# Sign words of float64 weights on GpSimd: high words times 0.0 in place of a comparison

## The chip, the core and the metric

The kernel runs on one core of a Trainium2 chip. The metric is the device time in microseconds (us) of one execution. The engines are TensorE (PE, with its weight loads as PEld), VectorE (DVE), ScalarE (ACT), GpSimd (POOL) and SyncE (SP), which issues nearly all DMAs. Each engine takes its instructions in the order in which they stand in its own queue.

## The reference

```python
scores = q @ k.T / sqrt(64)                    # 4 batches x 8 heads, 576 x 576, head_dim 64
bias   = -(cum[:, None] - cum[None, :])        # cum: running sum of max(s, 0)
scores = where(causal, -1e9, scores + minimum(bias, 0))
x   = softmax(scores) @ v                      # to 2304 tokens x 512
h   = x @ w_in;  x = (h * clip(h + 3, 0, 6) / 6) @ w_out        # 512 -> 2048 -> 512
h   = x @ w2_in; out = (h / (1 + exp(-h))) @ w2_out             # 512 -> 2048 -> 512
```

The four weight matrices arrive as float64. [...]

## The kernel before, in words

Attention runs by head: 22 heads are done "whole" in one float32 matmul, the others with operands split into a high part and a remainder. Each of the two feed-forward layers multiplies with split operands as well: a product is high*high + high*low + low*high, three matmuls in a row (lines 260 to 262 and 299 to 301 in the first layer, 1013 to 1015 and 1029 to 1031 in the second).

Weights come in chunks of 128 x 512 values, two `in` and `out` chunks (`i`, `o`) for each of 16 slices of a layer. A `Chunk` goes through these steps: `load` (L147, a DMA of 128 x 1024 words into the tile `raw`); `fields`, where ACT shifts the low word (L159) and makes the magnitude (L160, tile `mag`, three buffers) and POOL makes the sign word in place of the high word (L161); `join`, where DVE shifts the magnitude and sets the sign (L172) and adds the low word (L176); then the split in a high part (ACT, L120) and a remainder (DVE, L187, which frees the `mag` buffer). All 64 chunks take L161. The high words that it reads and writes lie 8 bytes apart, since low and high words alternate in `raw`. For the `i` chunks of the second layer `Two` takes two chunks together, forms sums of them (L915), splits these too (L925, L927) and stores all in DRAM.

The first layer's gates are on ACT (L272) and DVE (L273), the high part `gh` of the gated values is a copy on POOL (L114) or, at the start, on DVE (L122), and its remainder `gl` is DVE's (L280). In the second layer DVE adds partial products (L1079, tiles `u` and `h`) out of the accumulator banks that PE then writes anew.

The program has three stretches that matter here: an opening (up to about 150 us), in which attention heads and the first layer's weight chunks share DVE and PE; the body, in which PE is fed without a break; and the change from the first layer to the second (about 540 to 650 us), in which DVE prepares the second layer's weights beside the last gates.

The order of instructions within each engine isn't the order of the code. A scheduler replays the whole program with its own cost for each instruction and fixes the queues by that. So a cheaper or dearer instruction moves others, on all engines.

Of the kernel before, what the change touches and what calls it, by code (L numbers as in the profile page):

```python
# [14 lines left out]
ALU = mybir.AluOpType  # L15
# [4 lines left out]
SIGN = -(2**31)  # L20


def f32(ap):
    return ap.bitcast(F32)
# [3 lines left out]
def kernel(  # L28
# [59 lines left out]
    def heads_of(x):  # L88
# [8 lines left out]
        out=cmask[:, NZ:], in_=cmask[:, NZ:], pattern=[[-1, P]],  # L97
# [32 lines left out]
    class Chunk:  # L130
# [20 lines left out]
        def fields(self):  # L151

            self.mag = stage.tile([P, DM], I32, tag="mag", name=f"mag{self.nm}")
            if self.src.dtype == F32:
                nc.scalar.copy(f32(self.mag), self.val)
                self.val = f32(self.mag)
                return
            low, high = self.words
            nc.scalar.activation(low, low.bitcast(U32), AF.Copy, scale=2.0**-29)  # L159
            nc.scalar.activation(f32(self.mag), f32(high), AF.Abs, scale=2.0**-112)  # L160
            nc.gpsimd.tensor_scalar(  # L161
                out=high, in0=f32(high), scalar1=0.0, scalar2=float(SIGN),
                op0=ALU.is_lt, op1=ALU.mult,
            )

        def join(self):
# [166 lines left out]
    def bank(kind, shape, name):  # L333
# [11 lines left out]
        out=srow, in0=srow, scalar1=0.0, scalar2=1.0 / SCALE, op0=ALU.max, op1=ALU.mult  # L345
# [876 lines left out]
```

## Time and profile before

| what | value |
|---|---|
| three runs, median (lowest to highest) | 1017.48 us (1015.5 to 1018.98) |
| the profiled execution | 1021.31 us, its span 1019.5 us |
| mean granted clock of TensorE | 0.991 of full speed |
| busy: PE, PEld, DVE, ACT, POOL | 989.4, 912.1, 715.0, 521.3, 340.5 us |
| L161 on POOL | 64 instructions, 69.5 + 68.8 us |

The span runs from the first instruction to the last; 1.8 us of the profiled execution lie around it. Busy time is the sum of an engine's instructions without overlaps. Matmul ends are modelled, so a PE that reads as busy can still run below its best rate; the number of matmuls in a stretch shows more. Spans on POOL are rough.

### The profile page before, as it was taken

How to read it: one execution, taken by the hardware profiler on the slowest of the kernel's cores; microseconds unless marked ns; L12 is line 12 of the kernel's file. 1: busy time of each engine (PE TensorE's matmuls, PEld its weight loads, DVE VectorE, ACT ScalarE, POOL GpSimd, SP SyncE). 2: the span in 40 equal slices, each digit the busy share in tenths (PEclk: the TensorE clock that was granted, in tenths of full speed). 3: DMA queues.
4: the chain of work that ended last, by engine and by line, in shares of the span. 5: the costliest groups of instructions: out<-in, count | busy, mean ns of one | idle time of the engine just before them, and what ended most of it. 6: DMA issues, size and time to landing. Idle time of an engine off the chain costs nothing.

```text
span 1019.5 us, 18411 instructions
## 1 busy us (share of the span) xinstructions
PE 989.4 (97%) x6404; PEld 912.1 (89%) x6404; DVE 715.0 (70%) x1724; ACT 521.3 (51%) x1144; POOL 340.5 (33%) x446
## 2 busy tenths in 40 slices
PE   8988989999999999999999999899999999999997
PEld 5788989999999999999998887789988999888996
DVE  5798998878778888887737799867574334743343
ACT  5798655555556566566526565546353232532232
POOL 7376754453245444444415366423000000000000
PEclk9998999999999999999999999999999999999999
DMA  4686112212312322322114965443354341432411
GB/s 153 197 286 225 38 37 83 74 57 59 91 57 65 92 58 68 94 59 67 59 42 136 380 247 175 146 186 114 145 189 165 132 144 74 177 137 110 145 73 62
DMA packets 52068, 124.80 MB, mean 122 GB/s; under 512 B 10004, under 2 KB 31752, under 8 KB 48648
## 3 DMA queue, kind: packets, MB, share of 16 engines
q1 hardware_dynamic: 51528, 122.97, 35.6%
q8 instruction: 51, 0.84, 0.3%
q10 hardware_dynamic: 448, 0.66, 0.2%
q14 instruction: 41, 0.34, 0.1%
HBM read 98.96 MB, written 24.63 MB: 121 GB/s over the span
## 4 chain that ended last, share of the span: by engine, by line
PE 78%; DVE 12%; ACT 3%; DMA 2%; POOL 2%; issue 2%; DVEq 0%; POOLq 0%; ACTq 0%; SPq 0%
PE a L1029 6%; PE a L1030 6%; PE a L1031 6%; PE h L1013 5%; PE h L1014 5%; PE h L1015 5%; PE acc L300 5%; PE ph L260 5%; PE acc L301 5%; PE acc L299 5%; PE ph L262 5%; PE ph L261 5%; PE poB L617 4%; PE pt0B L567 1%; DVE mago L172 1%
## 5 line engine op out<-in xcount | busy, mean ns | idle before, releaser
L300 PE MATMUL acc<-gl,wo 128*128 128x256 f32 (+1 forms) x512 | 155.0, 304 | 2.7 <-DVE gl L280 2.7
L260 PE MATMUL ph<-xh,wi 128*128 128x256 f32 (+1 forms) x512 | 152.8, 299 | 3.4 <-DVE g L273 3.4
L301 PE MATMUL acc<-gh,wo 128*128 128x256 f32 (+1 forms) x512 | 152.7, 300 | 0.0
L262 PE MATMUL ph<-xh,wi 128*128 128x256 f32 (+1 forms) x512 | 151.3, 296 | 0.6 <-DVE wi L187 0.6
L261 PE MATMUL ph<-xl,wi 128*128 128x256 f32 (+1 forms) x512 | 150.9, 295 | 0.0
L299 PE MATMUL acc<-gh,wo 128*128 128x256 f32 (+1 forms) x512 | 145.2, 301 | 3.1 <-DVE gh L122 3.1
L1071 ACT ACTIVATE gh<-h 128x384 fp32r<-128x384 f32 x96 | 50.3, 524 | 187.7 <-DVE h L1079 187.6
L1029 PE MATMUL a<-wo,gh 128*128 128x512 f32 x288 | 113.5, 394 | 2.6 <-ACT gh L1071 2.5
L1030 PE MATMUL a<-wo,gh 128*128 128x512 f32 x288 | 113.5, 394 | 0.0
L300 PEld LDWEIGHTS acc<-gl,wo 128*128 128x128 f32 x512 | 97.9, 191 | 8.1 <-DVE gl L280 4.9
L260 PEld LDWEIGHTS ph<-xh,wi 128*128 128x128 f32 x512 | 97.0, 190 | 7.1 <-DVE g L273 2.3
L299 PEld LDWEIGHTS acc<-gh,wo 128*128 128x128 f32 x512 | 96.4, 191 | 7.1 <-ACT magi L160 2.5
L301 PEld LDWEIGHTS acc<-gh,wo 128*128 128x128 f32 x512 | 97.9, 191 | 3.6
L262 PEld LDWEIGHTS ph<-xh,wi 128*128 128x128 f32 x512 | 97.0, 189 | 3.8 <-DVE wi L187 0.8
L261 PEld LDWEIGHTS ph<-xl,wi 128*128 128x128 f32 x512 | 96.9, 189 | 2.9
L161 POOL TENSOR_SCALAR rawi<-rawi 128x512 int32<-128x512 f32 x32 | 68.8, 2150 | 76.9 <-ACT magi L160 57.1
L1031 PE MATMUL a<-wo,gl 128*128 128x512 f32 x288 | 90.0, 393 | 0.3 <-DVE gl L1073 0.3
L161 POOL TENSOR_SCALAR rawo<-rawo 128x512 int32<-128x512 f32 x32 | 69.5, 2176 | 44.2 <-ACT mago L160 41.1
L1073 DVE TENSOR_TENSOR gl<-h,gh 128x384 fp32r<-128x384 f32 x96 | 53.6, 558 | 40.7 <-ACT h L1072 39.1
L1079 DVE TENSOR_TENSOR h<-h,u 128x384 f32<-128x384 f32 x72 | 40.1, 557 | 54.8 <-PE h L1015 54.6
L273 DVE SCALAR_TENSOR_TENSOR g<-g,ph 128x512 f32<-128x512 f32 (+1 forms) x76 | 49.5, 652 | 34.5 <-ACT g L272 34.3
L272 ACT ACTIVATE g<-ph,half 128x512 f32<-128x512 f32 (+1 forms) x76 | 50.3, 662 | 37.9 <-PE ph L262 37.2
(232 smaller groups left out, 2655.8 us busy)
## 6 DMA issues: line engine op xcount, KB each, us to landing
w<-w_d SPq DMA_DIRECT2D x18, 1792.0 KB
w_d<-w SPq DMA_DIRECT2D x8, 1792.0 KB
k2B<-in_kT_dram SPq DMA_DIRECT2D x64, 144.0 KB
rawi<-in_w1i_dram SPq DMA_DIRECT2D x16, 512.0 KB
rawo<-in_w1o_dram SPq DMA_DIRECT2D x16, 512.0 KB
rawi<-in_w2i_dram SPq DMA_DIRECT2D x16, 512.0 KB
rawo<-in_w2o_dram SPq DMA_DIRECT2D x16, 512.0 KB
q2B<-in_qT_dram SPq DMA_DIRECT2D x64, 80.0 KB
```

The lines of the kernel that those rows point to most:

```text
L161: nc.gpsimd.tensor_scalar(out=high, in0=f32(high), scalar1=0.0, scalar2=float(SIGN), op0=ALU.is_lt, op1=ALU.mult,)
L260: nc.tensor.matmul(o, wih[:, cs], xh[c], start=c == 0, stop=False)
L261: nc.tensor.matmul(o, wih[:, cs], xl[c], start=False, stop=False)
L262: nc.tensor.matmul(o, wil[:, cs], xh[c], start=False, stop=c == NDC - 1)
L299: nc.tensor.matmul(a, woh[:, cs], gh[:, jj, :], start=b0, stop=False)
L300: nc.tensor.matmul(a, woh[:, cs], gl[:, jj, :], start=False, stop=False)
L301: nc.tensor.matmul(a, wol[:, cs], gh[:, jj, :], start=False, stop=b1)
L1013: nc.tensor.matmul(ps, w[:, 0, cs], xh[:, c, :], start=c == 0, stop=False)
L1029: nc.tensor.matmul(accs[t], gh[:, k, cs], woh, start=b0, stop=False)
L1030: nc.tensor.matmul(accs[t], gh[:, k, cs], wol, start=False, stop=False)
L1031: nc.tensor.matmul(accs[t], gl[:, k, cs], woh, start=False, stop=b1)
L1073: nc.vector.tensor_tensor(out=gl[:, i, o], in0=g, in1=f32(gh[:, i, o]), op=ALU.subtract)
```

## The change

One instruction changes its arithmetic and its output type. Before, it compared the high word, read as float32, with 0.0 and multiplied the outcome by -2^31, written as an integer. Now it multiplies the high word by 0.0 and by 1.0 and writes float32: a zero that keeps the sign, whose bit pattern is the same sign word.

```diff
             nc.gpsimd.tensor_scalar(
-                out=high, in0=f32(high), scalar1=0.0, scalar2=float(SIGN),
-                op0=ALU.is_lt, op1=ALU.mult,
+                out=f32(high), in0=f32(high), scalar1=0.0, scalar2=1.0,
+                op0=ALU.mult, op1=ALU.mult,
             )
```

No instruction is added or removed, but the queues are ordered anew: in the opening and in the change of layers; the rest stays as it was.

DVE in the opening, before. `pb` and `mx` are scores and maxima of attention heads, `sums` their row sums, `magi_0`, `mago_0`, `magi_1` the first weight chunks:

```order
L545 RECIPROCAL sums_127<-sums_127 128x2
L544 TENSOR_SCALAR sums_129<-sums_129 128x2
L545 RECIPROCAL sums_129<-sums_129 128x2
L524 ISA pb0A_2_233,mxA_2_232<-ps0A_2_246,cmask 128x128
L524 ISA mxA_2_232 128x1
L524 ISA pb1A_2_234,mxA_2_232<-ps1A_2_249,cmask 128x256
L524 ISA mxA_2_232 128x1
L172 SCALAR_TENSOR_TENSOR magi_0_271<-magi_0_271,rawi_0_172 128x512
L176 ISA magi_0_271<-rawi_0_172,magi_0_271 128x1024
```

DVE at the same place, now:

```order
L172 SCALAR_TENSOR_TENSOR magi_0_271<-magi_0_271,rawi_0_172 128x512
L545 RECIPROCAL sums_127<-sums_127 128x2
L172 SCALAR_TENSOR_TENSOR mago_0_398<-mago_0_398,rawo_0_174 128x512
L176 ISA magi_0_271<-rawi_0_172,magi_0_271 128x1024
L544 TENSOR_SCALAR sums_129<-sums_129 128x2
L172 SCALAR_TENSOR_TENSOR magi_1_508<-magi_1_508,rawi_1_176 128x512
L524 ISA pb0A_2_233,mxA_2_232<-ps0A_2_246,cmask 128x128
```

The joins of three chunks, each of which waits for its L161, now stand ahead of the third head's scores; before, the first of them stood behind these scores and the other two further on.

DVE in the change of layers, before. `gl_9195` is the last remainder of the first layer, `o_0` and `o_2` take its sums out of their banks, `u_0_0_9312` and `h_0_0_9321` are the first additions of the second layer, `mago_8` to `mago_12` its `out` chunks:

```order
L280 TENSOR_TENSOR gl_9195<-g_9193,gh_9194 128x512
L176 ISA mago_7_9397<-rawo_7_9221,mago_7_9397 128x1024
L187 TENSOR_TENSOR wo_6_9406<-mago_6_9386,wo_6_9406 128x512
L187 TENSOR_TENSOR wo_7_9540<-mago_7_9397,wo_7_9540 128x512
L172 SCALAR_TENSOR_TENSOR mago_8_9408<-mago_8_9408,rawo_8_9382 128x512
L122 COPY o_0_9235<-acc_1_8613 128x512
L176 ISA mago_8_9408<-rawo_8_9382,mago_8_9408 128x1024
L122 COPY o_2_9240<-acc_3_8615 128x512
L172 SCALAR_TENSOR_TENSOR mago_9_9542<-mago_9_9542,rawo_9_9393 128x512
L187 TENSOR_TENSOR wo_8_9551<-mago_8_9408,wo_8_9551 128x512
L1079 TENSOR_TENSOR u_0_0_9312<-h_2_9305,p_0_0_9296 128x384
```

DVE ahead of the same first addition, now:

```order
L172 SCALAR_TENSOR_TENSOR mago_11_9681<-mago_11_9681,rawo_11_9415 128x512
L172 SCALAR_TENSOR_TENSOR mago_12_9692<-mago_12_9692,rawo_12_9549 128x512
L176 ISA mago_11_9681<-rawo_11_9415,mago_11_9681 128x1024
L187 TENSOR_TENSOR wo_10_9690<-mago_10_9553,wo_10_9690 128x512
L176 ISA mago_12_9692<-rawo_12_9549,mago_12_9692 128x1024
L122 COPY o_0_9235<-acc_1_8613 128x512
L122 COPY o_2_9240<-acc_3_8615 128x512
L187 TENSOR_TENSOR wo_11_9845<-mago_11_9681,wo_11_9845 128x512
L187 TENSOR_TENSOR wo_12_9854<-mago_12_9692,wo_12_9854 128x512
L172 SCALAR_TENSOR_TENSOR magi_8_9705<-magi_8_9705,rawi_8_9701 128x512
L176 ISA magi_8_9705<-rawi_8_9701,magi_8_9705 128x1024
L1079 TENSOR_TENSOR u_0_0_9312<-h_2_9305,p_0_0_9296 128x384
```

The first addition moved from place 1362 of DVE's queue to place 1375: thirteen more instructions of weight preparation stand ahead of it.

## Rows read from the trace of the kernel before

**Rows 1.** The page: busy time of each engine, its share and instructions.

```profile
PE 989.4 (97%) x6404; PEld 912.1 (89%) x6404; DVE 715.0 (70%) x1724; ACT 521.3 (51%) x1144; POOL 340.5 (33%) x446
```

**Rows 2.** Windows: stretch, length, busy (count) of PE, PEld, DVE, ACT, POOL, clock, DMA share, GB/s.

```profile
60.00:70.00 10.00, 7.42 (x56) 6.43 (x54) 10.00 (x35) 10.00 (x28) 7.04 (x7) 1.00 0.74 240
80.00:90.00 10.00, 8.09 (x39) 7.70 (x39) 7.88 (x17) 7.26 (x15) 7.81 (x6) 0.66 0.80 290
130.00:140.00 10.00, 7.63 (x50) 7.28 (x51) 9.94 (x22) 5.30 (x13) 8.59 (x7) 0.87 0.22 61
170.00:180.00 10.00, 10.00 (x85) 9.87 (x83) 7.54 (x23) 5.25 (x13) 4.06 (x9) 1.00 0.22 65
...
570.00:580.00 10.00, 10.00 (x44) 8.05 (x44) 5.52 (x11) 4.81 (x8) 2.89 (x2) 1.00 1.00 399
610.00:620.00 10.00, 9.57 (x42) 7.42 (x41) 10.00 (x14) 6.08 (x10) 5.74 (x4) 1.00 0.40 129
640.00:650.00 10.00, 7.30 (x25) 5.50 (x24) 9.63 (x19) 6.69 (x13) 5.76 (x3) 0.83 0.76 266
650.00:660.00 10.00, 10.00 (x50) 8.93 (x49) 7.15 (x16) 3.23 (x7) 2.93 (x2) 1.00 0.29 102
```

**Rows 3.** Groups on POOL by shape: count, busy us, mean ns, idle before.

```profile
L161 POOL TENSOR_SCALAR rawo<-rawo 128x512 int32<-128x512 f32 x32 | 69.5, 2176 | 44.2 <-ACT mago L160 41.1 <-DMA q2A<-in_qT_dram 1.4 <-DMA k2A<-in_kT_dram 1.0
L161 POOL TENSOR_SCALAR rawi<-rawi 128x512 int32<-128x512 f32 x32 | 68.8, 2150 | 76.9 <-ACT magi L160 57.1 <-PE h L1015 12.0 <-issue 6.4
L114 POOL TENSOR_SCALAR gh<-g 128x512 fp32r<-128x512 f32 x68 | 49.6, 729 | 56.6 <-DVE g L273 54.1 <-DVE sums L545 1.9
```

**Rows 4.** Waits, whole span: total us, times, longest us.

```profile
DVE gl L280 <- POOL gh L114: 8.1, 13, 1.0
DVE magi L172 <- POOL rawi L161: 7.6, 4, 3.5
```

**Rows 5.** The chain that ended last: start us, us, what.

```profile
98.05 2.01 POOL rawi L161
...
562.71 8.21 DMA rawi<-in_w2i_dram
...
572.35 1.98 POOL rawi L161
...
581.98 2.00 POOL rawi L161
...
592.84 2.00 POOL rawo L161
```

**Rows 6.** Timeline of DVE and POOL, 98 to 110 us: start, length, [idle before].

```profile
100.08 1.09 DVE L172 SCALAR_TENSOR_TENSOR magi<-magi,rawi 128x512 int32<-128x512 int32 x1 [1.16 <-POOL rawi L161]
105.20 0.67 DVE L172 SCALAR_TENSOR_TENSOR mago<-mago,rawo 128x512 int32<-128x512 int32 x1
105.81 1.10 DVE L187 TENSOR_TENSOR wi<-magi,wi 128x512 fp32r<-128x512 f32 x1
107.78 1.13 DVE L172 SCALAR_TENSOR_TENSOR magi<-magi,rawi 128x512 int32<-128x512 int32 x1
...
105.64 0.73 POOL L114 TENSOR_SCALAR gh<-g 128x512 fp32r<-128x512 f32 x1
107.71 2.01 POOL L161 TENSOR_SCALAR rawo<-rawo 128x512 int32<-128x512 f32 x1 [1.35 <-ACT mago L160]
```

**Rows 7.** Groups on DVE in the weight preparation, as in rows 3.

```profile
L172 DVE SCALAR_TENSOR_TENSOR magi<-magi,rawi 128x512 int32<-128x512 int32 x32 | 24.8, 775 | 7.6 <-POOL rawi L161 7.6
L176 DVE CUSTOM_DVE_ANT_0 mago<-rawo,mago 128x1024 uint16<-128x1024 uint16 x32 | 24.3, 761 | 0.0
```

**Rows 8.** Groups on PE, the page: which waits precede the line.

```profile
L300 PE MATMUL acc<-gl,wo 128*128 128x256 f32 (+1 forms) x512 | 155.0, 304 | 2.7 <-DVE gl L280 2.7
```

**Rows 9.** Timeline, the change of layers: first product on PE, first addition on DVE.

```profile
630.91 0.45 PE L1013 MATMUL h<-x0b,w 128*128 128x384 f32 x1 [0.80 <-ACT o L120]
634.15 0.54 DVE L1079 TENSOR_TENSOR u<-h,p 128x384 f32<-128x384 f32 x1
```

## The prediction

> **What bounds the kernel now.** I read the busy times first, then the windows, then the waits and the chain, and last the instructions around the changed one. The busy times show PE at 989.4 us, 97% of the span, and POOL, on which the change lies, at 340.5 us, 33% [rows 1]. POOL is never what the whole kernel waits for; a faster POOL can only help where another engine waits for it and PE waits for that engine. So the question is where PE isn't fed. The windows show it by the number of matmuls [rows 2]. At 170 us PE does 85 in 10 us with no idle time, in the body's mix of shapes. At 60 us it does 56, at 80 us 39, at 130 us 50: measured by 85, these three windows lose 10 x (29 + 46 + 35) / 85 = 12.9 us. In two of them, 60 and 130 us, DVE is busy for 10.00 and 9.94 of 10 us, so DVE sets the pace there. In the change of layers PE does 44 of its larger matmuls at 570 us and is fed; at 640 us it does 25 where the next window has 50, a loss of 5.0 us, with DVE busy for 9.63. The clock follows: 0.66, 0.87 and 0.83 of full speed in the windows at 80, 130 and 640 us, so part of each ran at the lower level of 1.2 GHz, after PE had stood idle. The loss that the change can reach is thus about 18 us in these windows, and it belongs to DVE first and to POOL only through DVE.
>
> **The instruction itself.** L161 takes 2.15 us on `i` chunks and 2.18 us on `o` chunks, 64 times [rows 3]. The new form, two float32 multiplications by constants, is what L114 does on the same 128 x 512 elements in 0.73 us [rows 3], but there the words are contiguous, and here they lie 8 bytes apart. No POOL row has this spacing without the comparison. So the bounds are 0.73 us, if the comparison and the integer output cost the time, and 2.16 us, if the spacing does; I allow no time below 0.73 us, as L114 has the same work on an easier layout, and none much above 2.16, as the layout stays. I take 0.73, the nearest row by operation. That saves 1.43 us each, 92 us of POOL's busy time, nearly all of it beside other work: POOL stands idle for 77 + 44 us ahead of L161 anyhow, mostly for ACT's magnitude [rows 3].
>
> The Trainium skill ("GPSIMD Engine Reference", section 7) puts its penalty for spread reads at steps above 8 bytes, with about 1.9 cycles per element below it; at that page's 1.2 GHz this is an estimate of 0.81 us for 512 elements. By it the saving would be 86 us of POOL in place of 92. No run here yet shows a spaced float32 copy.
>
> **The opening.** Three terms.
> First, waits of DVE for the sign words. They come to 7.6 us in 4 cases in the whole span [rows 4], and only one of these stands in the opening's chain, 1.16 us ahead of L172 at 100 us [rows 5, 6]. With L161 shorter by 1.43 us that wait goes: -1.2 us, and what comes last then is ACT's magnitude or DVE itself.
> Second, `gh` of the gates stands on POOL behind L161, and DVE waits for it 13 times, 8.1 us [rows 4]; PE in turn waits 2.7 us for `gl` [rows 8]. I take half of these 2.7 us: -1.4, between 0 and -2.7.
> Third, DVE slows down beside POOL. L172 takes 0.67 us alone and 1.13 us where an L161 begins with it; L187 takes 1.10 us beside an L114 of only 0.73 us [rows 6]. The loss is about 0.4 us for one meeting, whether the POOL instruction is long or short. Over all, L172 on `i` chunks has a mean of 775 ns and L176 on `o` chunks 761 [rows 7], so 32 x (0.105 + 0.091) = 6.3 us are lost in these two of the preparation's six groups, at most 3 x 6.3 = 19 us in all, part of it beside L114. If each meeting costs 0.4 us, a shorter L161 meets DVE somewhat less often, not three times less. I take -3.5 us, -2.5 in the opening and -1 in the change of layers; the bounds are 0 and -10, about half of the 19.
> On the page's side ("GPSIMD Engine Reference", section 1) POOL shares its SBUF interfaces with DVE, in contention with DVE instructions of two SBUF inputs. The rows agree as to which instructions suffer. Read as a loss in proportion to the time of overlap, the rule would give about -10 us in place of -3.5; read as a loss per meeting, 0. The L187 row beside the short L114 speaks for the second.
> The new order puts the joins of the first chunks ahead of the third head's scores. That fills DVE early, where it is not full; but behind 50 us the same work of DVE stands in the same stretch, so I count it at nothing, with +-3 us. If the sign word were late, the scores behind the join would wait, and PE's transposes behind these.
> Sum of the opening: -1.2 - 1.4 - 2.5 = -5.1 us, nearly all on the path, as DVE is full there.
>
> **The body** keeps its order, and PE is fed: 0. **The second layer** behind 650 us is fed as well (50 matmuls in the window at 650 us) and POOL soon has nothing to do: 0.
>
> **The change of layers.** The chain runs through three L161 at 572, 582 and 593 us [rows 5], ahead of the stretch in which DVE is full. Each gives 1.43 us: DVE gets its work 4.3 us earlier, which the idle 4.5 us of DVE at 570 us can take up [rows 2]. Against that stands the new order: thirteen more instructions of preparation ahead of the first addition of the second layer, at about 0.7 us each (0.67 alone, 0.76 to 0.78 on average [rows 6, 7]), 9.1 us. Net, with -1 from contention: 9.1 - 4.3 - 1.0 = +3.8 us on DVE, so this addition, at 634.15 us before, comes at about 638. PE has other work meanwhile: its first product began at 630.91 us [rows 9], and eight products of six matmuls fit in its banks, 48 matmuls at 10/50 = 0.2 us each [rows 2], until about 640.5 us. The first addition is thus still in time, but those behind it are later too, and PE waited for them before. I let +1.5 us of the 3.8 reach PE, between 0 and +9.
>
> **Sum.** -5.1 + 1.5 = -3.6 us on the profiled execution's 1021.3 us (span 1019.5 and 1.8 around it), which gives 1017.7. That execution is 3.8 us above the median of the runs shown, so on the median of 1017.5 I predict 1014.0 us. What a measurement of this kernel can tell from no change is 0.3%, or 3 us.
>
> **Rivals.**
> 1. Hidden anyway. DVE's own work sets both stretches and contention costs per meeting, so that only the link at 98 us and some of the `gh` waits are left: -2 us in the opening, taken back by +2 in the change of layers. For it: POOL idles ahead of L161 far more than anyone waits behind it [rows 3, 4]. Against it: POOL is busy 7 to 9 of 10 us in the opening's windows [rows 2]. Time 1017.
> 2. The change of layers gets slower. Mechanism: DVE takes its queue in order, and the second layer's first additions, and thus PE's free banks, stand behind joins of chunks whose words come late. The DMA of a chunk took 8.21 us in the chain, with the DMA engines full at 570 us [rows 2, 5], and a faster POOL doesn't move that. It decides once chunks `o`11, `o`12 and `i`8 are joined later than about 640 us. Then the 9.1 us come through whole and PE stands still for them, and a longer idle time brings more of the lower clock (the 0.83 at 640 us is 1.7 us of lost work in 10). With 9.1 + 1.7 - 5.1 of the opening, and without the links' gain, it is +5.7 us: 1023.
> 3. The instruction isn't faster. If the spacing costs the 2.16 us, the queues rely on a sign word that comes 1.4 us later than planned. Joins now stand ahead of scores in the opening and ahead of additions in the change of layers; if eight of the 64 make a full engine wait, that is 8 x 1.4 = +11 us less what POOL's idle time lends; I take half: +5.6, 1023. For it: no row shows spaced words with a float32 result. Against it: a factor of three between two instructions of one kind asks for more than layout.
> 4. More than I count: if contention goes in proportion to L161's time, -10 in place of -3.5, a time of 1007.5.
>
> **How the numbers follow.** The forecast with rival 4, faster by more than 0.3%: 0.45 (0.37 and 0.08). Rival 1, within 0.3%: 0.30. Slower: 0.25, rival 2 with 0.16 and rival 3 with 0.09. The forecast's own range, with the bounds of its terms, is 1007 to 1014.4. The range for 8 in 10 has to take in rivals 1 and most of 2 and 3: 1005 to 1023.
>
> **What would show it.** L161 as float32 at 0.7 to 0.9 us and POOL's busy time near 250 us: the first step is right; at 2 us rival 3 holds. No wait of DVE for L161 near 98 us, and waits of `gl` for `gh` below 8.1 us: the second. Means of L172 and L176 below 0.76 us: the third. More matmuls than 56, 39 and 50 in the windows at 60, 80 and 130 us would be the opening's gain; fewer than 25 at about 640 us, or a first addition after 640 us, the loss in the change of layers. The forecast is wrong if the windows of the opening hold as many matmuls as before, or if PE's first products wait longer than they did.

## The result and the profile after

The change makes the kernel slower: 1025.53 us against 1018.18 (medians of six runs each), a ratio of 1.0069 with a 95% interval of 1.005 to 1.0089. A second measurement, beside the experiments, gave 1.008 (1.0056 to 1.0104). 1014.0 was predicted, with 1005 to 1023 as the range. The profiled execution of the changed kernel took 1024.4 us, its span 1022.6.

The page of the changed kernel, busy times, and the groups of its POOL [rows 1, 3]:

```profile
PE 988.6 (97%) x6404; PEld 909.5 (89%) x6404; DVE 716.7 (70%) x1724; ACT 522.1 (51%) x1144; POOL 261.6 (26%) x446
```

```profile
L114 POOL TENSOR_SCALAR gh<-g 128x512 fp32r<-128x512 f32 x68 | 51.2, 753 | 77.2 <-DVE g L273 72.9 <-PE acc L301 2.5 <-DVE sums L545 1.1
L161 POOL TENSOR_SCALAR rawo<-rawo 128x512 f32<-128x512 f32 x32 | 30.0, 940 | 64.5 <-ACT mago L160 61.0 <-DMA rawo<-in_w1o_dram 3.5
L161 POOL TENSOR_SCALAR rawi<-rawi 128x512 f32<-128x512 f32 x32 | 25.3, 794 | 109.4 <-ACT magi L160 80.1 <-PE h L1015 28.9 <-POOL q2A L407 0.2
```

The instruction did what was asked of it: 0.79 and 0.94 us in place of 2.15 and 2.18, and POOL has 79 us less to do. The busy times of PE, DVE and ACT are within 2 us of what they were.

Windows of the changed kernel, columns as in [rows 2]:

```profile
60.00:70.00 10.00, 8.93 (x69) 8.16 (x68) 10.00 (x35) 9.93 (x27) 3.65 (x7) 1.00 0.82 271
80.00:90.00 10.00, 7.06 (x56) 6.39 (x54) 9.81 (x29) 7.71 (x18) 3.32 (x7) 1.00 0.93 287
130.00:140.00 10.00, 9.72 (x84) 9.55 (x83) 9.38 (x21) 6.49 (x16) 7.55 (x8) 1.00 0.06 18
...
620.00:630.00 10.00, 7.23 (x25) 5.46 (x24) 9.49 (x16) 6.41 (x11) 4.13 (x4) 0.83 0.34 108
640.00:650.00 10.00, 3.80 (x14) 2.64 (x13) 7.70 (x17) 4.97 (x10) 1.33 (x1) 0.79 0.82 313
650.00:660.00 10.00, 10.00 (x45) 8.82 (x44) 4.74 (x9) 2.52 (x5) 0.65 (x1) 0.87 0.14 41
```

The opening's three windows hold 69, 56 and 84 matmuls for 56, 39 and 50 before [rows 2], and look like a gain. The window at 640 us holds 14 for 25: that is the loss. Its size is read from where the same instructions start. First the kernel before, then the changed one: the first product of the first layer's last block (L260), in the changed kernel also the first of the second layer (L1013), and last the 24th matmul of L1029.

```profile
535.81 1.10 PE L260 MATMUL ph<-xh,wi 128*128 128x512 f32 x4
...
671.24 0.39 PE L1029 MATMUL a<-wo,gh 128*128 128x512 f32 x1
```

```profile
532.71 1.10 PE L260 MATMUL ph<-xh,wi 128*128 128x512 f32 x4
...
629.86 0.33 PE L1013 MATMUL h<-x0b,w 128*128 128x384 f32 x1
...
674.76 0.39 PE L1029 MATMUL a<-wo,gh 128*128 128x512 f32 x1
```

At the first of these the changed kernel is 3.1 us ahead; at the second layer's first product, L1013, 1.05 us (629.86 for 630.91 [rows 9]); at the 24th matmul of L1029 it is 3.5 us behind (674.76 for 671.24), and 3.1 at the end. So between 533 and 675 us it loses 6.6 us.

What happens there, in the changed kernel's waits of PE from 600 to 690 us (columns as in [rows 4]):

```profile
PE a L1029 <- ACT gh L1071: 5.7, 1, 5.7
PE acc L299 <- POOL gh L114: 2.8, 1, 2.8
```

Of the 5.7 us, the timeline of ACT, DVE and PE, and a piece of the chain (start, length, what):

```profile
636.31 0.56 DVE L1079 TENSOR_TENSOR u<-h,p 128x384 f32<-128x384 f32 x1 [1.48 <-ACT p L1088]
...
643.85 0.55 DVE L1079 TENSOR_TENSOR h<-h,u 128x384 f32<-128x384 f32 x1
...
647.34 0.66 ACT L159 ACTIVATE rawi<-rawi 128x512 int32<-128x512 uint32 x1 [2.70 <-DMA rawi<-in_w2i_dram]
647.90 0.51 ACT L1071 ACTIVATE gh<-h 128x384 fp32r<-128x384 f32 x1
...
648.46 0.80 PE L1029 MATMUL a<-wo,gh 128*128 128x512 f32 x1 [5.70 <-ACT gh L1071]
```

```profile
640.73 6.59 DMA rawi<-in_w2i_dram
647.32 0.02 issue
647.34 0.66 ACT rawi L159
648.00 0.42 ACT gh L1071
```

The third gate of the second layer's first step (L1071) has its sum from VectorE at 644.40 us (643.85 + 0.55). It begins at 647.90, because in ScalarE's queue L159 stands ahead of it, the first treatment of weight chunk `i`11, and that waits for a DMA issued at 640.73 us. In the kernel before, SyncE issued the DMAs of `i`10 and `i`11 from 648.61 us on only, and both L159 stood behind all four gates. There VectorE's sum was no earlier (its addition began at 644.05 us and took 0.55), but the gate began at once. The rows of this gate, of PE's wait and of the first L159:

```profile
644.64 0.52 ACT L1071 ACTIVATE gh<-h 128x384 fp32r<-128x384 f32 x1 [0.87 <-DVE h L1079]
...
645.21 0.50 PE L1029 MATMUL a<-wo,gh 128*128 128x512 f32 x1 [2.33 <-ACT gh L1071]
...
652.70 0.67 ACT L159 ACTIVATE rawi<-rawi 128x512 int32<-128x512 uint32 x1 [2.85 <-DMA rawi<-in_w2i_dram]
```

### The profile page after: what moved, and what is told of

It is laid out like the page before. It is cut to its first block, busy times and chain, and to the rows that moved or that the text cites. A ratio compares the mean times of both kernels' runs of the same rounds, so it can differ in the third digit from the quotient of the medians.

```text
span 1022.6 us, 18425 instructions
## 1 busy us (share of the span) xinstructions
PE 988.6 (97%) x6404; PEld 909.5 (89%) x6404; DVE 716.7 (70%) x1724; ACT 522.1 (51%) x1144; POOL 261.6 (26%) x446
## 4 chain that ended last, share of the span: by engine, by line
PE 79%; DVE 9%; DMA 5%; POOL 2%; issue 2%; SPq 2%; ACT 1%; POOLq 0%; DVEq 0%; ACTq 0%
PE a L1029 6%; PE a L1030 6%; PE a L1031 6%; PE h L1013 5%; PE h L1014 5%; PE h L1015 5%; PE acc L300 5%; PE ph L260 5%; PE ph L262 5%; PE acc L301 5%; PE ph L261 5%; PE acc L299 5%; PE poB L617 4%; PE pt0B L567 1%; DVE mago L172 1%
## 5 line engine op out<-in xcount | busy, mean ns | idle before, releaser
L260 PE MATMUL ph<-xh,wi 128*128 128x256 f32 (+1 forms) x512 | 152.2, 298 | 2.3 <-DVE g L273 2.3
L1071 ACT ACTIVATE gh<-h 128x384 fp32r<-128x384 f32 x96 | 50.4, 525 | 192.0 <-DVE h L1079 191.8
L1029 PE MATMUL a<-wo,gh 128*128 128x512 f32 x288 | 113.8, 395 | 5.9 <-ACT gh L1071 5.9
L260 PEld LDWEIGHTS ph<-xh,wi 128*128 128x128 f32 x512 | 96.6, 189 | 6.8 <-DVE g L273 1.7
L1079 DVE TENSOR_TENSOR h<-h,u 128x384 f32<-128x384 f32 x72 | 40.1, 557 | 56.5 <-PE h L1015 56.2
L114 POOL TENSOR_SCALAR gh<-g 128x512 fp32r<-128x512 f32 x68 | 51.2, 753 | 77.2 <-DVE g L273 72.9
L1029 PEld LDWEIGHTS a<-wo,gh 128*128 128x128 f32 x288 | 54.5, 189 | 15.2 <-ACT gh L1071 6.9
```

The costliest lines, as they stand in the source:

```text
L114: nc.gpsimd.tensor_scalar(out=o, in0=i, scalar1=1.0, scalar2=1.0, op0=ALU.mult, op1=ALU.mult)
L260: nc.tensor.matmul(o, wih[:, cs], xh[c], start=c == 0, stop=False)
L1029: nc.tensor.matmul(accs[t], gh[:, k, cs], woh, start=b0, stop=False)
```

## The experiments

The change has two effects that can be taken apart: the instruction is faster, and the scheduler, which sees that, orders the queues anew. Most kernels below exchange the sign-word instruction only after the scheduler has fixed the queues, so that the order and the instruction can be chosen apart. By the instructions' order in the traces, the changed kernel's queues differ from those before up to about 263 us and again between about 537 and 726 us; "opening" below means the first of these two stretches, which is longer than the 150 us named above.

```diff
     with _tile.TileContext(nc, schedule_with_timeline_sim=True) as tc:
         tile_attention_moe_moe_kernel(tc, *args)
+    for fn in nc.m.functions:
+        for bb in fn.blocks:
+            for n, x in enumerate(bb.instructions):
+                if ...:                            # the 64 instructions of L161
+                    bb.instructions[n] = _replace(x, op0=ALU.mult, ...)
```

All results, as ratios to the kernel before (four_forms, further down, ran once and serves for the time of single instructions only):

| run | sign word | order of the opening | order of the change of layers | ratio (95%) |
|---|---|---|---|---|
| changed kernel | new | new | new | 1.0069 (1.005 to 1.0089) |
| after_again | new | new | new | 1.008 (1.0056 to 1.0104) |
| new_op_old_order | new | old | old | 0.9973 (0.9953 to 0.9993) |
| new_op_old_again | new | old | old | 0.9988 (0.9965 to 1.001) |
| old_op_new_order | old | new | new | 1.0321 (1.0299 to 1.0343) |
| new_op_new_opening | new | new | old | 1.0004 (0.9987 to 1.0022) |
| new_op_new_change | new | old | new | 1.003 (1.0011 to 1.005) |
| gates_before_field | new | new | new, one tie on ACT | 1.0036 (1.0016 to 1.0057) |
| gate_before_joins | new | new | new, one tie on DVE | 1.002 (0.9997 to 1.0043) |
| new_order_before_64us | new | a third | old | 1.0059 (1.0041 to 1.0078) |
| new_order_behind_64us | new | a fourth | old | 0.9994 (0.9969 to 1.0019) |
| order_for_slower | new | a fifth | a third | 1.0293 (1.0264 to 1.0322) |

### The instruction or the order

**new_op_old_order**, the exchange above on the kernel before.

> The order of every queue is that of the kernel before; all 64 sign-word instructions are the new ones (put in once the scheduler has run). Theory A (the order of the queues costs the 7.3 us, and not the instruction: the new order gains 3.1 us in the opening and loses 6.6 at the change of layers): with the old order neither, so 1016.5 to 1018.5 us, at most 1.5 us below the kernel before by the shorter waits of VectorE for L161. Theory B (the fast instruction itself does harm, wherever it stands): about 1025. Theory C (the gain of the opening is the instruction's, the loss is the order's): 3 us below the kernel before, about 1015.

1017.61 us, 0.9973. That is 2.4 us below the kernel before in the same series: beyond what theory A allowed (at most 1.5), nearest to C (3 us), and far from B. Its groups on VectorE, and its waits for POOL:

```profile
L172 DVE SCALAR_TENSOR_TENSOR magi<-magi,rawi 128x512 int32<-128x512 int32 x32 | 24.0, 751 | 1.5 <-POOL rawi L161 1.5
L176 DVE CUSTOM_DVE_ANT_0 mago<-rawo,mago 128x1024 uint16<-128x1024 uint16 x32 | 23.7, 741 | 0.0
```

```profile
DVE gl L280 <- POOL gh L114: 7.6, 12, 1.0
DVE magi L172 <- POOL rawi L161: 1.5, 2, 0.8
```

In the old order the waits for L161 fall from 7.6 to 1.5 us, and L172 on `magi` and L176 on `mago` are 24 and 20 ns shorter on average [rows 4, 7].

**new_op_old_again**, the same once more.

> The new instruction in the old order once more, beside the three that follow. All theories: 0.995 to 0.9995 of the kernel before.

0.9988, with an interval that passes 1. The two together say about 0.998, some 2 us, in one measurement told from nothing and in the other not. By its ratios it is the fastest version that was run.

**old_op_new_order**, the other way round: the changed kernel's queues with the comparison.

> The order of every queue is that of the changed kernel; all 64 sign-word instructions are the old comparison. Theory A: 1024 to 1027 us, as the changed kernel, or up to 1.5 us above it since each sign word is 1.4 us later. Theory B: as the kernel before, about 1018. Theory C: 1028 to 1029, the loss of the order without the gain of the instruction.

1053.24 us, 33 us above the kernel before; no theory had it. VectorE's waits:

```profile
DVE magi L172 <- POOL rawi L161: 23.4, 20, 2.8
DVE mago L172 <- POOL rawo L161: 10.3, 15, 2.0
```

These are 33.7 us where the kernel before has 7.6 on `magi` [rows 4] and 0.4 on `mago`. The new order has put joins where a sign word of 2.2 us comes too late, 35 times; with the short one the same order still waits 4.6 us on `magi` and 2.1 on `mago`, the old order 1.5 in all. So the new order gives away the shorter waits that the instruction brings in the old one.

**new_op_new_opening** and **new_op_new_change**: the scheduler saw the new instruction in one layer's chunks and the comparison in the other's; then the 32 comparisons were exchanged.

```diff
-                out=high, in0=f32(high), scalar1=0.0, scalar2=float(SIGN),
-                op0=ALU.is_lt, op1=ALU.mult,
+                out=(high, f32(high))[self.key[1] == 0], ...       # 1 for the other kernel
+                op0=(ALU.is_lt, ALU.mult)[self.key[1] == 0], op1=ALU.mult,
```

> All 64 sign-word instructions are the new ones. In the first layer the queues stand as in the changed kernel, and from the change of layers on as in the kernel before (its scheduler saw the new instruction in the first layer's chunks and the comparison in the second's). Theory A: the opening's gain of 3.1 us without the loss: about 1015 us. Theory B: about 1025. Theory C: about 1015, the same as the old order with the new instruction.

> All 64 sign-word instructions are the new ones. In the first layer the queues stand as in the kernel before, and from the change of layers on as in the changed kernel. Theory A: the loss of 6.6 us alone, about 1024 to 1025 us, with a wait of TensorE for ACT's gate L1071 of 4 to 6 us near 645 us, as in the changed kernel. Theory B: about 1025. Theory C: 3 us of the instruction's gain stay, about 1021 to 1022.

1.0004 and 1.003. From the 0.998 of the new instruction in the old order, the new order costs 0.24% in the opening and 0.50% at the change of layers, 2.4 and 5 us; with the instruction's -2 the sum is +5.4 us, of the 7 and 8 measured. The 5 us are clear of the intervals; the 2.4 us are at their edge (the intervals of 1.0004 and of 0.9973 overlap). So the loss at the change of layers is the order's, as theories A and C both said, and the wait for L1071 is there, 4.9 us. The 1015 us that both had for the new opening did not come.

The gain of 3.1 us in the opening, on which theory A rested, was none. A second profiled execution of the same changed kernel (after_again, below) starts the last block's first product where the kernel before does, at 535.81 us:

```profile
535.80 1.10 PE L260 MATMUL ph<-xh,wi 128*128 128x512 f32 x4
```

What differs is the clock: over the first 150 us its mean was 0.95 in the profile of the kernel before, 0.99 in the first of the changed kernel and 0.97 in the second. In the windows at 80 and 130 us it was 0.66 and 0.87 in the kernel before [rows 2] and 1.00 in the changed one, so at most 10 x (0.34 + 0.13) = 4.7 us of work that the one execution lost there and the other did not. How much this varies shows in the runs of the kernel before, 1014.64 to 1024.35 us in one series of 29; over these, 0.001 of mean clock goes with 0.96 us.

### The waits at the change of layers

**after_again**, the changed kernel itself, beside the next two.

> The changed kernel once more, beside the two that follow. All theories: 1.005 to 1.009 of the kernel before, as the first time.

1.008, as expected; its PE waits 5.5 us for L1071 and 2.2 for L114.

**gates_before_field**: one tie, all else left to the scheduler. The two L159 of chunks `i`10 and `i`11 moved behind the four gates; by the traces the queue of POOL stayed as it was, those of PE and DVE but for a few neighbours behind 655 us.

```diff
+            lastgate[b, q] = nc.scalar.activation(g, src, AF.Silu).ins
...
-                pair(q + 2)
+                with tc.issue_after(lastgate[0, 0]) if q + 2 == 5 else ExitStack(): pair(q + 2)
```

> The changed kernel with one tie: on ScalarE the work on the chunks i10 and i11 of layer two (L159) may not stand ahead of the four gates (L1071) of the second layer's first step. PE, POOL, SP and DVE keep their order but for one pair of neighbours. Theory D (two instructions that wait at the head of a queue make the loss at the change of layers; the larger is L159, which waits on ScalarE for its DMA in front of the gates): the wait of PE L1029 for ACT gh L1071 near 645 us falls from 5.7 us to 2.5 or less, and the time by 3 to 5 us, to 1.002 to 1.004 of the kernel before. Rival E (the gates come late whatever stands in front of them, since VectorE's additions L1079 are late): the wait stays, and the time is that of the changed kernel.

1.0036, 4.4 us below the changed kernel of the same series. Its timeline, and its window at 640 us:

```profile
648.25 0.51 ACT L1071 ACTIVATE gh<-h 128x384 fp32r<-128x384 f32 x1
...
648.81 0.50 PE L1029 MATMUL a<-wo,gh 128*128 128x512 f32 x1 [2.35 <-ACT gh L1071]
...
650.97 1.24 ACT L159 ACTIVATE rawi<-rawi 128x512 int32<-128x512 uint32 x2
```

```profile
640.00:650.00 10.00, 6.51 (x29) 4.71 (x28) 9.79 (x20) 5.87 (x11) 2.78 (x3) 1.00 0.69 251
```

PE's wait is 2.35 us, as in the kernel before (2.33), and both L159 come later at no cost that shows. The window holds 29 matmuls for 14, but this execution reaches the stretch 3.7 us later than the changed kernel's (L1013 for the first time at 633.66 us, for 629.86), so the two windows don't hold the same work. The place of L159 in ScalarE's queue, an instruction of 0.66 us, made about half of the loss in time; rival E falls. (The tie holds both chunks; the L159 that holds up the gate is that of `i`11.)

**gate_before_joins**: on VectorE, the joins of `o`6 and later behind the last gate of layer one.

```diff
-        nc.vector.scalar_tensor_tensor(
+        W['g'] = nc.vector.scalar_tensor_tensor(
             out=g, in0=g, scalar=1.0, in1=ph, op0=ALU.min, op1=ALU.mult
-        )
+        ).ins
...
-                self.ch[t - 1].join()
+                with tc.issue_after(W['g']) if self.ch[0].key[1] and t - 1 >= 6 else ExitStack(): self.ch[t - 1].join()
```

> The changed kernel with another tie: on VectorE the joins of chunk o6 and of all later ones may not stand ahead of the last gate of layer one (L273 of g75). With it the scheduler also puts L159 of i10 behind the first step's gates. Theory D: both waits go (PE L299 for POOL gh L114 near 625 us, 2.8 us; PE L1029 for ACT gh L1071, 5.7 to about 2.3), and the time falls by 5 to 7 us, to 0.9995 to 1.002 of the kernel before, near that of the run with the new opening and the old change of layers (1.0004). Rival E: the joins come later, second-layer weights are late in turn, and the time stays within 2 us of the changed kernel.

1.002, at the upper end of theory D; by the ratios 6 us below the changed kernel (by the medians 7.3). The last gate, its high part and the products that wait for it, and two windows:

```profile
622.87 0.69 DVE L273 SCALAR_TENSOR_TENSOR g<-g,ph 128x512 f32<-128x512 f32 x1 [4.35 <-ACT g L272]
...
623.72 0.93 POOL L114 TENSOR_SCALAR gh<-g 128x512 fp32r<-128x512 f32 x1 [5.92 <-DVE g L273]
...
624.70 1.19 PE L299 MATMUL acc<-gh,wo 128*128 128x512 f32 x4
```

```profile
620.00:630.00 10.00, 8.63 (x36) 6.22 (x35) 7.13 (x12) 4.87 (x9) 0.93 (x1) 1.00 0.40 139
640.00:650.00 10.00, 6.51 (x26) 5.05 (x25) 10.00 (x18) 6.47 (x13) 2.53 (x4) 0.88 0.75 267
```

VectorE now stands idle ahead of the gate (4.35 us) and PE doesn't wait for its high part: 36 matmuls for 25 at 620 us and 26 for 14 at 640, where the kernel before has 25. With this tie the scheduler also put the L159 behind the gates and moved much else from 609 us on, so the run undoes both waits together; new waits of PE stand beside that, 1.9 us for an addition (L1079) and 1.2 for `gl`. The difference to the run before, 0.16% or 1.6 us, lies within the intervals, and the mean clock of the runs differs with it (0.9949 for 0.9919).

The same stretch in all these traces, in us, shows what each order costs there, apart from what the opening did to the execution:

| run | first product of the last block | 24th matmul of L1029 | between |
|---|---|---|---|
| kernel before | 535.81 | 671.24 | 135.43 |
| new_op_old_order | 535.71 | 669.10 | 133.39 |
| changed kernel | 532.71 | 674.76 | 142.05 |
| after_again | 535.80 | 678.42 | 142.62 |
| new_op_new_change | 530.04 | 670.09 | 140.05 |
| gates_before_field | 536.46 | 673.25 | 136.79 |
| gate_before_joins | 534.95 | 671.45 | 136.50 |

With the same instruction, the changed order takes 6.7 (new_op_new_change) to 9.2 us longer here than the old one. The tie on ScalarE alone takes 5.3 to 5.8 us off the changed kernel's stretch. The tie on VectorE takes off no more than 0.3 us beyond that, so what the wait for the last gate costs is not shown, and what makes the 3.1 to 3.4 us that are left is open.

### What of the instruction cost the time

**four_forms**: the old order, and the sign words in four ways.

```diff
+                    if name.startswith("rawi0"):      # comparison and product, written as float32
+                    elif name.startswith("rawo0"):    # two products, written as int32
+                    elif name.startswith("rawi1"):    # the new instruction
```

> The order of every queue is that of the kernel before; the sign words are made in four ways, to see what part of the instruction costs. Layer 1, chunks i: comparison and product, written as float32 (the product is with 0.0, so the sign is left out). Layer 1, chunks o: two products, written as int32 (sign left out too). Layer 2, chunks i: the new instruction. Layer 2, chunks o: the old one. Theory F (the conversion to integers costs the 1.3 us): 0.7 to 0.9 us for layer 1 i, 2.0 to 2.2 us for layer 1 o. Theory G (the comparison costs it): the other way round. Both in part would lie between, say 1.4 us each.

Groups on POOL, first from 0 to 300 us (layer 1), then behind (layer 2):

```profile
L161 POOL TENSOR_SCALAR rawi<-rawi 128x512 f32<-128x512 f32 x16 | 35.1, 2193 | 32.0 <-ACT magi L160 27.3 <-DMA inA<-in_qT_dram 4.4
L161 POOL TENSOR_SCALAR rawo<-rawo 128x512 int32<-128x512 f32 x16 | 13.0, 816 | 26.4 <-ACT mago L160 15.1 <-DMA rawi<-in_w1i_dram 6.4 <-DMA k2A<-in_kT_dram 2.7
...
L161 POOL TENSOR_SCALAR rawo<-rawo 128x512 int32<-128x512 f32 x16 | 35.0, 2196 | 25.2 <-ACT mago L160 25.2
L161 POOL TENSOR_SCALAR rawi<-rawi 128x512 f32<-128x512 f32 x16 | 12.4, 775 | 68.1 <-ACT magi L160 43.4 <-PE h L1015 13.0 <-issue 9.1
```

Theory G, without remainder: the comparison with a product costs 2.19 to 2.20 us whatever it writes, and two products 0.78 to 0.82, as float32 or as integers.

### Are orders better with more slack?

Since the order made for the fast instruction lost, an order made for a slower one might win. Two kernels let the scheduler see the fast instruction in a part of the first layer's chunks (`self.key[2] < 6`, and `>= 6`), a third made it see a slower one (`out=self.raw, in0=f32(self.raw)`, all 1024 columns); all 64 were exchanged afterwards.

> All 64 sign words by the new instruction. The scheduler saw it in the chunks 0 to 5 of layer one alone (their sign words start up to 64 us) and the comparison in the rest: the opening gets another order, the change of layers stands as in the kernel before. Theory S (an order made for a faster instruction has less slack, and the chip takes it back): between the old order with the new instruction and that with the new opening, 0.9973 to 1.0004. Theory L (every order of the opening is a draw, some us better or worse, whatever instruction it was made for): anywhere from 0.993 to 1.006, with no regard to how many chunks were seen as fast.

> The same with the chunks 6 to 15 of layer one seen as fast, and 0 to 5 with the comparison. Theory S: between 0.9973 and 1.0004 again. Theory L: 0.993 to 1.006. Where one of the two halves is as slow as the whole new opening and the other as fast as the old one, the loss lies in that half.

> All 64 sign words by the new instruction, in an order that was made for one slower than the comparison (1024 columns in place of 512 while the scheduler looked). Theory S: more slack still, so no slower than the old order with the new instruction: 0.994 to 0.998. Theory L: a draw for the opening and one for the change of layers, 0.993 to 1.01; above 1.001 it would speak against S.

1.0059, 0.9994 and 1.0293. Theory S falls with the first, which lies outside its range, and again with the third: PE now waits for weights that come too late in the queues.

```profile
PE ph L260 <- ACT wi L120: 10.9, 5, 3.1
```

These 10.9 us are a part of the loss of about 30. The loss lies ahead of the last block, whose first product starts at 562.95 us for 535.81; from there to the 24th matmul of L1029 this order takes 133.2 us, no more than the old one. Theory L holds for the opening, where orders made for different mixes of the same two durations, all run with the same instruction, lie between 0.9973 and 1.0059; for the third kernel it was too narrow as well. Which instructions pay in the opening's new order isn't settled: PE's waits there differ by 1 to 2 us in many places, and two single profiles don't tell them from the clock.

## Why the prediction was wrong

Two of its steps failed. The larger miss is the opening, forecast at -5.1 us and about +0.4 by the runs (-2 and +2.4). The other is the share of the change of layers that reaches PE, forecast at +1.5 us and about +5 by the runs, which made the kernel slower and not merely no faster.

- **The instruction** was foreseen well, mis-sized a little: 0.86 us on average, (30.0 + 25.3) / 64, for 0.73, so 83 us of POOL's work saved in place of 92. Rival 3 is out. The Trainium skill ("GPSIMD Engine Reference", section 7), from whose 1.9 cycles per element the prediction estimated 0.81 us, was nearer. The products of four_forms agree (0.82 and 0.78 us).
- **The opening**, forecast at -5.1 us, is the first step that failed. In the old order about -2 came, from the instruction, for the whole kernel. Of the three terms, the waits for L161 fell as forecast in the old order (7.6 to 1.5 us); in the changed kernel's own order 4.6 and 2.1 us of them are left, one of 0.9 us at 94 us. The waits of `gl` for `gh` hardly fell: 7.6 us in the old order, and in the changed kernel they rose, 9.7 for 8.1 [rows 4]. Contention was -3.5 in the forecast; L172 on `magi` and L176 on `mago` had means of 769 and 757 ns in the changed kernel for 775 and 761 [rows 7], so 0.3 us in the two groups, and VectorE's busy time as a whole rose from 715.0 to 716.7 us. That the loss is one per meeting was right: of the 176 instructions on L172, L176 and L187, 28 took over 0.9 us in the kernel before, and 25 in the changed kernel as well as in new_op_old_order. The size of -3.5 did not follow from it.
- **The new order of the opening** was counted "at nothing, with +-3 us": it cost 2.4 by the runs, at the edge of what they can tell, and with that the rest of the forecast gain.
- **The step that made the kernel slower** is "I let +1.5 us of the 3.8 reach PE". The order at the change of layers cost about 5 us by the runs (6.6 in the profile). It was inside the bounds of the term, 0 to +9, but the working looked at VectorE's queue alone. There it was not far off: the first addition came at 636.31 us, 2.2 later than before and well before the 640 that were to decide, and PE's banks didn't wait for it. Even this delay was not that of the thirteen instructions ahead: VectorE stood idle 1.48 us for ScalarE's L1088, which stood behind an L159 that had waited 2.37 us for its own DMA. The wait that cost the time stood on ScalarE too, whose queue the prediction never read: a chunk's L159 that had moved ahead of the gates, behind a DMA of 6.59 us. A smaller one, 2.2 to 2.8 us, was VectorE's, but at the last gate of the layer before, not at the first addition; what it cost is not shown.
- **Rival 2** had the sign and the place, and half of the mechanism: a queue taken in order that stands at an instruction whose chunk comes late by DMA while PE needs the one behind it. It had the wrong engine and the wrong point of decision. That its price (1023) is near is luck: it is the sum of 9.1 us on VectorE and a gain of 5.1 in the opening, and neither came. Its sign in the profile, "fewer than 25 at 640", came true with 14.
- **The opening's windows**, named as the proof of a gain, showed more matmuls and proved nothing. They hold 64, 53 and 63 in new_op_old_order too, for 56, 39 and 50, and there the last block starts at 535.71 us for 535.81. The loss of 12.9 us that the prediction read from them is by the same working 8.8 us in that trace, with nothing gained.
- **The range** was too narrow for its own terms. Their bounds (-1.2; 0 to -2.7; 0 to -10; +-3; 0 to +9) give about 1001 to 1028 us and not "1007 to 1014.4", so the measured 1025.53 lay inside the bounds and outside the 1023 that was named. The sum itself gives 1013.9, written as 1014.0.

## What to carry to other kernels

Where a scheduler orders the queues by its own costs, a faster instruction off the critical path can be, as here, a small gain of its own and a new order of much else; price the order by reading, on every engine, what now stands ahead of the work that feeds the bound engine, instructions that wait for a DMA above all. Such a change is best tried with the instruction exchanged after the scheduling, which tells the two effects apart in one run. And a gain of 3 us between two profiles is no gain until their clocks have been compared, or until a second execution of the same kernel shows it; windows are compared only where the same instructions stand in them.

## What the runs showed of the hardware that was not expected

- On GpSimd a comparison with a product costs 2.19 us on 128 x 512 elements that lie 8 bytes apart, and two products 0.78 to 0.82 us on the same, with integers or floats written: the operation sets the time, not the conversion.
- VectorE's weight preparation lost time to an L161 only where its instruction began just behind the start of the L161. In the kernel before, 62 instructions of L172, L176 and L187 ran beside one L161 and nothing else of POOL. Of these, 15 began at most 0.6 us behind the L161's start, and took 1.05 us on average. The 35 that began later in it, up to 2.2 us behind its start, took 0.66 to 0.69 us, as did the 12 that began ahead of it. So making L161 1.3 us shorter took away time in which VectorE was not slowed.
- The comparison put into an order made for the short instruction cost 33 us in time, and VectorE's waits for it grew from 8.0 to 33.7 us. How many of these waits reached the end isn't shown: the mean clock fell as well, to 0.981 from 0.9926, which by 0.96 us for 0.001 goes with some 11 us (an estimate).
- Where PE stood idle, part of the stretch was granted the lower level, 1.2 GHz. From 620 to 660 us the four windows of the changed kernel, in which PE waited 2.8 and 5.7 us, had 0.83, 1.00, 0.79 and 0.87 of full speed; those of the kernel with the gates first 1.00, 0.83, 1.00 and 1.00, and those of the kernel before 1.00, 1.00, 0.83 and 1.00. The runs of new_op_new_change had a mean clock of 0.9906, those of new_op_old_order 0.9931; by 0.96 us for 0.001 that is an estimate of 2.4 of the 5.5 us between their means (1023.1 and 1017.55). So a part of the loss, under a half by this, goes with a clock that was lower beside the waits.
